# A fused attention and feed-forward kernel: tiles of x and g at another place modulo 512 bytes, and a gate ahead of GpSimd's first sums

## The chip, the core and the metric

The kernel runs on one NeuronCore of a Trainium2 chip. The engines named here are PE (TensorE, the matrix unit), DVE (VectorE), ACT (ScalarE), POOL (GpSimd) and SP (SyncE, which issues every DMA of this kernel). Each has its own instruction stream, worked off in order; they wait for each other through semaphores. The metric is the time of one execution on the device in microseconds (us), the median of several runs.

## The reference

Attention within chunks of 64 tokens, and on its output a feed-forward layer with a gated activation. All inputs are float32, except that the weights come as float64 words to this kernel.

```python
scores = scale * np.matmul(q_c, k_c.transpose(0, 1, 2, 4, 3))     # 8 batches, 8 heads, 9 chunks of 64 x 64
attn = np.exp(scores - np.max(scores, axis=-1, keepdims=True))
attn = attn / (np.sum(attn, axis=-1, keepdims=True) + 1e-09)
x = np.matmul(attn, v_c)            # rearranged to 4608 tokens x 512
...
h = x @ w_in                        # 512 x 2048
g = h * (1.0 / (1.0 + np.exp(-1.702 * h)))
return (g @ w_out)                  # 2048 x 512
```

## The kernel before, in words

**Splitting.** A float32 product is made of three matmuls in the type fp32r: each operand is split into a high part (`_h`) and a low part (`_l`), and high by low, high by high and low by high are summed in PSUM. The traces show these operands as f32.

**Tiling.** The 4608 tokens are 9 blocks of 512 (index n), and the 2048 inner features 16 slices of 128 (index j). One step g = 16 n + j of the feed-forward is: h, 12 matmuls with a 128x128 piece of `w_in` as the stationary operand and 512 columns of x as the moving one (L1513 to L1515); GELU and the high part of g on ACT (L1537, L1538); its low part on DVE (L1543); then o, for each of four 128-token tiles three matmuls with 128 columns of g as the stationary operand and 512 columns of `w_out` as the moving one (L1553 to L1555). Steps 0 and 1 do h in two halves of 256 columns (L1526 to L1529).

**Stages.** Blocks 0 to 2 go this way. For blocks 3 to 8 the product with `w_in` is done two blocks at a time with seven products for eight (L820 to L822), on tiles that lie in the weights' old places; blocks 7 and 8 do the same for `w_out` (L1067 to L1069, 256 columns wide). Sums of `w_in` pieces for this are made on POOL (`whole` and `sums`, L699 to L709) and stored to a tensor in DRAM, from where they are loaded again later.

**Weights.** A slice j of both weights arrives as 8-byte words (`raw_j`, two DMAs of SP, L365 and L370), is turned into float32 by two passes on ACT (L374, L381) and two on DVE (L387, L394), and is split by ACT (L410) and DVE (L413). The result is one tile w_j of 8 KB in each partition. That goes on during blocks 0 and 1.

**Attention.** It runs beside the feed-forward, two 128-token tiles at a time: DVE transposes, 64x64 matmuls (L1293, L1367), softmax on DVE and ACT, and one multiplication on POOL (L1323).

**Order.** The order of all 2,693 steps is written out by name in the table `ORDER`; `Plan.emit` runs through it and issues the steps' instructions. Names: `h0_g` and `h_g` the halves of h, `gh_g` and `gl_g` the parts of g, `o_g_t` the output matmuls, `raw_j`, `wsc_j`, `wlow_j`, `wshift_j`, `wj_j`, `wh_j`, `w_j` the steps of a weight, `pa0_p`, `pa_p`, `psum_p` the sums on POOL. A step's `need` only asserts that the needed steps stand ahead of it in the table. What an engine waits for on the chip follows from the tiles that its instructions read and write.

**Places.** Tiles are laid out one behind the other in each partition. Of the kernel before, in bytes modulo 512: the tiles w_j begin at 128, x_h and x_l at 128, g_h and g_l at 128. Every piece of them that a matmul reads begins a multiple of 512 bytes further on.

Of the kernel before, what the change touches and what calls it, by code (L numbers as in the profile page):

```python
# [234 lines left out]
def tile_chunk_attention_ffn(  # L235
# [9 lines left out]
    nc = tc.nc  # L245
# [38 lines left out]
    ps_a = ctx.enter_context(tc.tile_pool(name="ps_a", bufs=1, space=bass.MemoryType.PSUM))  # L284

    ident = const.tile([P, P], F32, tag="ident", name="ident")
    make_identity(nc, ident)

    buffers = {b: 2 for b in ("hp", "att", "x", "ob")}
    buffers.update({f"w{j}": 1 for j in range(NF)})  # L290
# [1403 lines left out]
```

## Time and profile before

| | us |
|---|---|
| median of 3 runs (819.7 to 821.64) | 819.97 |
| the profiled execution | 821.13 |
| its span, from the first to the last instruction | 819.4 |

The trace gives each instruction's start and duration, and for an idle stretch of an engine what ended it. A matmul's duration includes the time its results take to drain, so durations of neighbours overlap; what a matmul costs in a row of them is the distance from its start to the next one's start. The chain that ended last is followed back from the end of the program, at each step to what released the instruction or to the one before it on its engine: what stands on it sets the end. The granted TensorE clock is 1.00 in every stretch of this execution.

### The profile page before, as it was taken

Reading aid. Unit: us, or ns where it says so; the run is one execution under the profiler, and the core shown is the slowest. Engines: PE = TensorE matmul, PEld = TensorE weight load, DVE = VectorE, ACT = ScalarE, POOL = GpSimd, SP = SyncE. Lnnn points to the kernel's source line nnn. Section 1 sums busy time; section 2 is a strip of 40 time slices with the busy share of each in tenths; the row PEclk is TensorE's granted clock in tenths of the full one; section 3 lists DMA queues with packets and bytes.
Section 4 is the critical chain, followed back from the end, with each engine's and each line's share of the span. In section 5 each row is a group of like instructions: output and inputs, shape, how many; then the busy total and the mean of one; then the engine's idle time right before and its main releaser. Section 6 shows DMA issues by size and latency. Waiting matters only on the chain.

```text
span 819.4 us, 15635 instructions
## 1 busy us (share of the span) xinstructions
PE 807.3 (99%) x6038; PEld 680.4 (83%) x6038; DVE 586.2 (72%) x865; ACT 383.5 (47%) x603; POOL 91.5 (11%) x82
## 2 busy tenths in 40 slices
PE   7899999999999999999999999999999999999998
PEld 6788878888888888888888888888888888889998
DVE  5788976356475879885698898776887454569852
ACT  5899824244355536423554352422565311267430
POOL 1000170000063661000001010000000000000000
PEclk9999999999999999999999999999999999999999
DMA  9998645353266677767666437686633047673433
GB/s 242 282 297 244 167 129 123 88 128 72 57 182 174 158 199 207 186 173 219 171 172 167 104 92 193 180 211 198 164 104 116 1 130 213 194 207 118 142 92 103
DMA packets 244010, 131.08 MB, mean 160 GB/s; under 512 B 187104, under 2 KB 211680, under 8 KB 243936
## 3 DMA queue, kind: packets, MB, share of 16 engines
q1 hardware_dynamic: 243936, 130.08, 58.6%
q8 instruction: 48, 0.79, 0.4%
q14 instruction: 26, 0.21, 0.1%
HBM read 97.52 MB, written 32.51 MB: 159 GB/s over the span
## 4 chain that ended last, share of the span: by engine, by line
PE 88%; DVE 4%; SPq 3%; ACT 2%; DMA 2%; issue 1%; DVEq 0%; ACTq 0%
PE po L1553 12%; PE po L1555 12%; PE po L1554 12%; PE hp L820 9%; PE hp L822 9%; PE hp L821 9%; PE hp L1515 4%; PE hp L1513 4%; PE hp L1514 4%; SPq L470 2%; PE s L1293 2%; PE x L1367 2%; DMA w<-seven 1%; DVE wtmp L394 1%; PE acc_X L1069 1%; PE acc_X L1068 1%
## 5 line engine op out<-in xcount | busy, mean ns | idle before, releaser
L1553 PE MATMUL po<-w,g_l 128*128 128x512 f32 x448 | 176.8, 395 | 0.6 <-DVE g_l L1543 0.5
L1555 PE MATMUL po<-w,g_h 128*128 128x512 f32 x448 | 174.5, 390 | 0.0
L1554 PE MATMUL po<-w,g_h 128*128 128x512 f32 x448 | 174.5, 389 | 0.0
L1553 PEld LDWEIGHTS po<-w,g_l 128*128 128x128 f32 x448 | 84.1, 188 | 20.1 <-DVE g_l L1543 1.9
L1555 PEld LDWEIGHTS po<-w,g_h 128*128 128x128 f32 x448 | 84.1, 188 | 17.7
L1554 PEld LDWEIGHTS po<-w,g_h 128*128 128x128 f32 x448 | 84.1, 188 | 16.8
L820 PE MATMUL hp<-w,w 128*128 128x512 f32 x224 | 87.6, 391 | 0.3 <-DMA w<-seven 0.2
L1342 DVE STREAM_TRANSPOSE eT<-e 32x512 f32<-32x512 f32 x120 | 84.2, 702 | 4.4 <-POOL e L1323 2.4
L822 PE MATMUL hp<-w,w 128*128 128x512 f32 x224 | 87.2, 389 | 0.0
L821 PE MATMUL hp<-w,w 128*128 128x512 f32 x224 | 87.1, 389 | 0.0
L1323 POOL TENSOR_TENSOR e<-e,r 128x1024 f32<-128x1024 f32 x16 | 31.2, 1953 | 437.8 <-DVE r L1320 365.0
L1513 PE MATMUL hp<-x_l,w 128*128 128x512 f32 x184 | 72.0, 391 | 0.0
L1515 PE MATMUL hp<-x_h,w 128*128 128x512 f32 x184 | 71.6, 389 | 0.0
L1514 PE MATMUL hp<-x_h,w 128*128 128x512 f32 x184 | 71.6, 389 | 0.0
L1543 DVE TENSOR_TENSOR g_l<-hp,g_h 128x512 fp32r<-128x512 f32 (+1 forms) x50 | 33.2, 664 | 51.9 <-ACT g_h L1538 51.8
L1537 ACT ACTIVATE hp<-hp 128x512 f32<-128x512 f32 (+1 forms) x50 | 28.4, 569 | 66.5 <-PE hp L1515 57.3
L820 PEld LDWEIGHTS hp<-w,w 128*128 128x128 f32 x224 | 42.0, 188 | 10.5 <-issue 1.1
L822 PEld LDWEIGHTS hp<-w,w 128*128 128x128 f32 x224 | 42.1, 188 | 8.8
L821 PEld LDWEIGHTS hp<-w,w 128*128 128x128 f32 x224 | 42.1, 188 | 8.6
L820 PE MATMUL hp<-w,pieces 128*128 128x512 f32 x112 | 43.8, 391 | 0.0
L822 PE MATMUL hp<-w,pieces 128*128 128x512 f32 x112 | 43.6, 389 | 0.0
L821 PE MATMUL hp<-w,pieces 128*128 128x512 f32 x112 | 43.6, 389 | 0.0
(237 smaller groups left out, 1558.6 us busy)
## 6 DMA issues: line engine op xcount, KB each, us to landing
w<-seven SPq DMA_DIRECT2D x112, 256.0 KB, 3.3
pieces<-seven SPq DMA_DIRECT2D x56, 256.0 KB, 3.4
seven<-w SPq DMA_DIRECT2D x24, 512.0 KB, 3.8
raw<-in_moe_w_in_dram SPq DMA_DIRECT2D x16, 512.0 KB, 5.9
raw<-in_moe_w_out_dram SPq DMA_DIRECT2D x16, 512.0 KB, 6.3
four<-four_w SPq DMA_DIRECT2D x32, 256.0 KB, 3.2
raw<-in_q_dram SPq DMA_DIRECT2D x208, 32.0 KB, 2.4
raw<-in_k_dram SPq DMA_DIRECT2D x208, 32.0 KB, 2.2
```

Source lines behind the costliest of these rows:

```text
L820: nc.tensor.matmul(hp, w[:, 0, c], xl[:, c], start=c == 0, stop=False)
L821: nc.tensor.matmul(hp, w[:, 0, c], xh[:, c], start=False, stop=False)
L822: nc.tensor.matmul(hp, w[:, 1, c], xh[:, c], start=False, stop=c == 1)
L1323: nc.gpsimd.tensor_tensor(st["e"], st["e"], bc(st["r"]), op=ALU.mult)
L1342: nc.vector.transpose(st["et"][po : po + 32, :, 32 * a : 32 * a + 32], st["e"][pi : pi + 32, :, 32 * b : 32 * b + 32],)
L1513: nc.tensor.matmul(hp, wh, xl, start=cc == 0, stop=False)
L1514: nc.tensor.matmul(hp, wh, xh, start=False, stop=False)
L1515: nc.tensor.matmul(hp, wl, xh, start=False, stop=cc == NCC - 1)
L1543: nc.vector.tensor_tensor(gl[:, c], hp, gh[:, c].bitcast(F32), op=ALU.subtract)
L1553: nc.tensor.matmul(po, gl[:, c], w[:, 0, :], start=first, stop=False)
L1554: nc.tensor.matmul(po, gh[:, c], w[:, 0, :], start=False, stop=False)
L1555: nc.tensor.matmul(po, gh[:, c], w[:, 1, :], start=False, stop=last)
```

## The change

Three things change.

1. Places. x tiles and g tiles get 64 bytes more than they use, and spacers of 64, 192 and 2 times 32 bytes are laid between pools of tiles. Bytes modulo 512 in the changed program: w_j as before at 128; x_h of the blocks 0 and 2 at 192, x_l of these at 256, x_h and x_l of block 1 at 320 and 384; the two buffers of g_h at 192 and 256, those of g_l at 320 and 384. Working tiles behind them (`wtmp`, `ob` and what shares their place) move to 448. The tiles of blocks 3 to 8 that lie in the weights' places stay at 128, and so do the loaded pieces.
2. A gate. One POOL instruction of a single column reads the low half of the last weight slice w_15; the first step of every pair's sums asks for it in the table, and on POOL all sums stand behind it.
3. The table `ORDER` is written anew, over all its length. The number of PE steps is the same.

```diff
@@ ORDER @@
-    "... hp0_8 o_13_3 gh_14 o_13_2 pa0_2 pout1_0 ... s_8 pa0_0 pout0_1 pa_0 ..."
+    "... hp1_8 w_15 gate s_8 qk_1_1_10 pa0_2 o_14_0 pout0_7 xh_7 pa0_0 ..."
@@ tile_chunk_attention_ffn @@
+    const.tile([P, 16], F32, tag="gap0", name="gap0")
...
+    def x_tile(tag, name):
+        t = const.tile([P, NCC * BT + 16], F32R, tag=tag, name=name)
+        return t[:, : NCC * BT].rearrange("p (n t) -> p n t", n=NCC)
+
+    def g_tile(w, name):
+        if "gap" not in held:
+            held["gap"] = two.tile([P, 8], F32, tag="gap2", name="gap2")
+        return two.tile([P, BT + 16], F32R, tag=f"g{w}", name=name)[:, :BT]
...
-        plan.add(POOL, 1.3, rank, lambda: whole(0), need=[w0, f"w_{NF - 1}"], make=e("pa0"), take=["tmp"])
+        plan.add(POOL, 1.3, rank, lambda: whole(0), need=[w0, "gate"], make=e("pa0"), take=["tmp"])
...
-                x_h[n] = const.tile([P, NCC, BT], F32R, tag=f"xe{2 * n % 4}", name=f"x_h_{n}")
-                x_l[n] = const.tile([P, NCC, BT], F32R, tag=f"xe{2 * n % 4 + 1}", name=f"x_l_{n}")
+                x_h[n] = x_tile(f"xe{2 * n % 4}", f"x_h_{n}")
+                x_l[n] = x_tile(f"xe{2 * n % 4 + 1}", f"x_l_{n}")
+                if n == 1:
+                    const.tile([P, 48], F32, tag="gap1", name="gap1")
...
-                gh = two.tile([P, BT], F32R, tag="gh", name=f"g_h_{g}")
-                gl = two.tile([P, BT], F32R, tag="gl", name=f"g_l_{g}")
+                gh = g_tile("h", f"g_h_{g}")
+                gl = g_tile("l", f"g_l_{g}")
...
+    def gate():
+        t = const.tile([P, P], F32, tag="gate", name="gate")[:, :1]
+        w = wt[NF - 1][:, 1, 1, :1].bitcast(F32)
+        nc.gpsimd.tensor_tensor(t, w, w, op=ALU.add)
...
+    plan.add(POOL, 0.12, -80, gate, need=[f"w_{NF - 1}"], make="gate")
```

POOL's own order, before, from the attention multiplication for tile 6 on; `e` is the softmax tile, `whole` and `sums` those of the weights' sums:

```order
L1323 TENSOR_TENSOR e_1019<-e_1019,r_1061 128x1024
L699 TENSOR_TENSOR whole_1301<-w_664 128x512
L699 TENSOR_TENSOR whole_1301<-w_716 128x512
L699 TENSOR_TENSOR whole_1383<-w_289 128x512
L699 TENSOR_TENSOR whole_1383<-w_448 128x512
L706 TENSOR_TENSOR sums_1400<-whole_1301 128x256
```

and in the changed program, where the line numbers are 10 to 18 higher:

```order
L1333 TENSOR_TENSOR e_1012<-e_1012,r_1057 128x1024
L1651 TENSOR_TENSOR gate<-w_1315 128x1
L709 TENSOR_TENSOR whole_1394<-w_670 128x512
L709 TENSOR_TENSOR whole_1401<-w_307 128x512
L709 TENSOR_TENSOR whole_1401<-w_449 128x512
L709 TENSOR_TENSOR whole_1394<-w_730 128x512
L716 TENSOR_TENSOR sums_1442<-whole_1394 128x256
```

The same four `whole` instructions of the pairs 2 and 0 now follow the gate, which reads w_15 (`w_1315`); before, nothing held them until w_15 was there.

SP's queue near the start, before; `raw_368` and `raw_385` are the words of the weights 2 and 3, `rows` the q and k of tile 4, `first_b` the v of tiles 2 and 3:

```order
L365 DMA raw_237<-in_moe_w_in_dram 128x4x128
L370 DMA raw_237<-in_moe_w_out_dram 128x512
L470 DMA rows_260<-in_q_dram 128x8x64
L470 DMA rows_260<-in_k_dram 128x8x64
L470 DMA first_b_245<-in_v_dram 128x8x64
L470 DMA first_b_314<-in_v_dram 128x8x64
L365 DMA raw_368<-in_moe_w_in_dram 128x4x128
L370 DMA raw_368<-in_moe_w_out_dram 128x512
```

and in the changed program:

```order
L366 DMA raw_236<-in_moe_w_in_dram 128x4x128
L371 DMA raw_236<-in_moe_w_out_dram 128x512
L480 DMA first_b_255<-in_v_dram 128x8x64
L480 DMA first_b_252<-in_v_dram 128x8x64
L366 DMA raw_329<-in_moe_w_in_dram 128x4x128
L371 DMA raw_329<-in_moe_w_out_dram 128x512
L480 DMA rows_359<-in_q_dram 128x8x64
L480 DMA rows_359<-in_k_dram 128x8x64
```

The words of weight 2 move ahead of the two loads of `rows`.

## Rows read from the trace of the kernel before

**Rows 1.** The page: busy us of each engine with its share of the span and its instructions; the granted clock in 40 equal slices, in tenths; the chain that ended last, by engine.

```profile
PE 807.3 (99%) x6038; PEld 680.4 (83%) x6038; DVE 586.2 (72%) x865; ACT 383.5 (47%) x603; POOL 91.5 (11%) x82
PEclk9999999999999999999999999999999999999999
PE 88%; DVE 4%; SPq 3%; ACT 2%; DMA 2%; issue 1%; DVEq 0%; ACTq 0%
```

**Rows 2.** The chain that ended last in order of time, in the stretches 20 to 40 us and 91 to 125 us: start us, us, what (`issue` is a wait for nothing the profile shows).

```profile
23.82 6.60 DMA raw<-in_moe_w_out_dram
...
103.53 2.23 DVE w L413
...
112.45 0.59 DVE g_l L1543
113.08 0.50 PE po L1553
113.58 0.23 PE po L1554
113.81 0.24 PE po L1555
```

**Rows 3.** The timeline of PE in the stretch 150 to 153 us: start us, us, engine, line, operation, out<-in, shapes (stationary, then output).

```profile
150.17 0.39 PE L1553 MATMUL po<-w,g_l 128*128 128x512 f32 x1
...
150.85 0.39 PE L1513 MATMUL hp<-x_l,w 128*128 128x512 f32 x1
...
152.89 0.39 PE L1513 MATMUL hp<-x_l,w 128*128 128x512 f32 x1
```

**Rows 4.** The same view at 740 us, where the matmuls are 256 columns wide.

```profile
740.09 0.28 PE L1067 MATMUL acc_Y<-w,w 128*128 128x256 f32 x1
...
741.89 0.28 PE L1067 MATMUL acc_Y<-w,w 128*128 128x256 f32 x1
```

**Rows 5.** The same view from 217 us, where o matmuls follow a block of 64x64 matmuls of the attention.

```profile
216.79 0.59 PE L1367 MATMUL x<-eT,v 64*64 64x64 f32 x28
217.31 0.50 PE L1553 MATMUL po<-w,g_l 128*128 128x512 f32 x1
217.65 0.39 PE L1554 MATMUL po<-w,g_h 128*128 128x512 f32 x1
217.88 0.40 PE L1555 MATMUL po<-w,g_h 128*128 128x512 f32 x1
218.12 0.39 PE L1553 MATMUL po<-w,g_l 128*128 128x512 f32 x1
218.34 0.40 PE L1554 MATMUL po<-w,g_h 128*128 128x512 f32 x1
218.58 0.39 PE L1555 MATMUL po<-w,g_h 128*128 128x512 f32 x1
218.81 0.39 PE L1553 MATMUL po<-w,g_l 128*128 128x512 f32 x1
```

**Rows 6.** The same view at 30 us, where h of the first step is done in halves of 256 columns.

```profile
30.30 0.28 PE L1528 MATMUL hp<-x_l,w 128*128 128x256 f32 x1
...
31.13 0.28 PE L1529 MATMUL hp<-x_h,w 128*128 128x256 f32 x1
```

**Rows 7.** Stretches of the span, for the instructions of L1553 alone (three rows) and of L1513 alone (two rows): stretch, its us, PE busy (instructions), PEld busy (instructions), granted clock, DMA share, GB/s.

```profile
22.00:113.00 91.00, 20.78 (x52) 9.76 (x52) 1.00 0.83 235
113.00:320.00 207.00, 54.98 (x139) 26.09 (x139) 1.00 0.53 135
320.00:700.00 380.00, 101.00 (x257) 48.24 (x257) 1.00 0.57 157
22.00:113.00 91.00, 20.61 (x52) 9.75 (x52) 1.00 0.83 235
113.00:320.00 207.00, 51.35 (x132) 24.78 (x132) 1.00 0.53 135
```

**Rows 8.** Stretches of the span, all engines: stretch, its us, busy us (instructions) of PE, PEld, DVE, ACT and POOL, granted clock, DMA share, GB/s.

```profile
40.00:80.00 40.00, 39.87 (x296) 32.34 (x295) 34.50 (x38) 37.59 (x46) 1.91 (x1) 1.00 0.99 274
113.00:320.00 207.00, 206.92 (x1739) 171.49 (x1740) 130.03 (x176) 90.94 (x138) 62.28 (x59) 1.00 0.53 135
320.00:640.00 320.00, 319.80 (x2292) 263.22 (x2291) 256.58 (x406) 141.30 (x239) 14.09 (x7) 1.00 0.60 163
```

**Rows 9.** The timeline of DVE (five rows), then of POOL (four rows), from 99 to 135 us.

```profile
99.69 1.23 DVE L394 CUSTOM_DVE_ANT_0 wtmp<-raw,wtmp 128x2048 uint16<-128x2048 uint16 x1
100.83 1.22 DVE L413 TENSOR_TENSOR w<-wtmp,w 128x1024 fp32r<-128x1024 f32 x1
...
103.53 2.23 DVE L413 TENSOR_TENSOR w<-wtmp,w 128x1024 fp32r<-128x1024 f32 x1
...
106.88 1.70 DVE L394 CUSTOM_DVE_ANT_0 wtmp<-raw,wtmp 128x2048 uint16<-128x2048 uint16 x1
...
112.95 1.20 DVE L413 TENSOR_TENSOR w<-wtmp,w 128x1024 fp32r<-128x1024 f32 x1
...
102.13 2.55 POOL L699 TENSOR_TENSOR whole<-w 128x512 f32<-128x512 f32 x2 [13.39 <-DVE w L413]
105.84 3.90 POOL L699 TENSOR_TENSOR whole<-w 128x512 f32<-128x512 f32 x2 [1.16 <-DVE w L413]
...
119.52 0.74 POOL L709 TENSOR_TENSOR sums<-whole,sums 128x256 f32<-128x256 f32 x1
...
133.47 1.90 POOL L1323 TENSOR_TENSOR e<-e,r 128x1024 f32<-128x1024 f32 x1 [10.60 <-ACT hp L1537]
```

More of the change, by code (lines that the diff above doesn't have):

```diff
@@ L865, in high @@
             g = (g1 if late else g0) + h
-            g_t[g] = [two.tile([P, BT], F32R, tag=f"g{w}", name=f"g_{w}_{g}") for w in "hl"]
+            g_t[g] = [g_tile(w, f"g_{w}_{g}") for w in "hl"]
             nc.scalar.activation(g_t[g][0], words(h, late), AF.Copy)
@@ L1022, in pair @@
             if r < 2:
-                return [two.tile([P, BT], F32R, tag=f"g{w}", name=f"c_{w}_{q}_{p}") for w in "hl"]
+                return [g_tile(w, f"c_{w}_{q}_{p}") for w in "hl"]
             t = wt[slots[r - 2]][:, 0]
```

344 rows, old and new, of the table ORDER are left out of this document.

## The prediction

> **What bounds the kernel now.** I read the page first: PE is busy in 99% of the span, 88% of the chain that ended last is PE's, and the granted clock is at its upper level in all 40 slices [rows 1]. So no engine beside PE can be the bound over the whole run; the time can only come out of the matmuls themselves, or out of the stage in which the chain is not PE's. Second, that chain in order of time: before 113.08 us it passes through the weights' words (a DMA of 6.60 us), ACT and DVE, for instance a split of w on DVE of 2.23 us; from 113.08 us on it is one matmul after the other [rows 2]. Third, the stretches: from 40 to 80 us the DMA engines are busy for 0.99 of the time and ACT for 37.59 of 40 us, from 113 us on DVE, ACT and POOL have room (130 of 207 us for DVE, 257 of 320 later) and the DMA share is 0.53 to 0.60 [rows 8]. A matmul that gets shorter after 113 us therefore shortens the run; one that gets shorter before mostly waits longer for its weight.
>
> Last, what a matmul costs. At 150 us twelve of them take 152.89 - 150.17 = 2.72 us, 226.7 ns each for 512 columns [rows 3]. At 740 us fifteen take 741.89 - 740.09 = 1.80 us, 120.0 ns each for 256 columns [rows 4]. The difference, 106.7 ns for 256 columns, is 0.417 ns per column, the upper clock level. What is left over is 13.3 ns per matmul at either width, though every one of them has another stationary operand. It is not quite constant: in the 256-column start of the kernel seven take 31.13 - 30.30 = 0.83 us, 118.6 ns each, a rest of 11.9 [rows 6], and after a break five take 218.81 - 217.65 = 1.16 us, 232 ns each, a rest of 18.7 [rows 5]. The columns cost the same in all three places, so something beside the columns, which depends on how a matmul stands to the weight load under it, costs 12 to 19 ns.
>
> **The change, part by part.** The sum is made against the profiled execution, 821.1 us; the median of the runs is 820.0, 1.2 lower.
>
> *Places.* In the kernel before, every stationary and every moving operand of a product has the same place modulo 512 bytes. The change pulls them apart for L1513 to L1515 (w against x) and L1553 to L1555 (g against w). After 113 us L1513 has 132 matmuls and L1553 139 + 257 [rows 7]; times three lines each, 3 x 528 = 1584. Before 113 us there are 3 x (52 + 52) = 312 more. The seven-products stage (L820 to L822, L1067 to L1069) keeps its places, so nothing is taken off there. No row of the kernel before has operands at two different places, so the price is bounded: at most the whole rest goes, 13.3 ns; at least nothing; and below nothing, since the 232 ns after a break show that the same operands can also run 5.3 ns slower than steady [rows 3, 5]. I take 8 ns, a bit over half of 13.3: the rest moves with the phase between load and columns, from 11.9 to 18.7, which speaks for two reads that get in each other's way, but a turn from an o matmul to an h matmul still loads w while w streams, and some fixed part for changing the weights may stay. 1584 x 8 ns = 12.7 us. On the 312 early ones I count nothing: DMA and ACT hide it [rows 8]. If that cover weren't there, they would be worth 312 x 8 ns = 2.5 us more.
>
> A rule of the Trainium skill bears on the size. Its page "TensorE: Matmul & The Clock Gate", section "Back-to-back issue gap", puts a matmul of a warm array at its columns over 2.4 GHz and about 2.5 ns, some 216 ns for 512 columns. The row says 226.7, so this kernel is 11 ns slower than that rule; were all of it the places' doing, the gain would be an estimated 17 us and the time about 801.
>
> *The gate.* POOL's `whole` additions run beside the weights' last passes. While they run, DVE's L413 takes 2.23 us against 1.22 just before, and L394 1.70 against 1.23 [rows 9]: 1.01 + 0.47 = 1.5 us, in the stretch where the chain goes through DVE. With the gate the sums start only after the last split (112.95 + 1.20 = 114.15 us) [rows 9]. Bounds are 0 and 1.5; I take 1.0, since part of a DVE stall there is found again as a wait for the next words. On the other side, POOL does four `whole` additions (2.55 us for two, undisturbed) and two rounds of sums behind the gate, where before only the sums stood there, which ended at 119.52 + 0.74 = 120.26. About 5.1 us later is 125.4, and POOL's next work, the multiplication of the attention, began at 133.47 after 10.60 us of idling [rows 9], so 8 us of cover are there; without it up to 5 us of attention delay would result, in a stage where PE has other steps. The gate itself is one column on an idle engine: nothing. The DVE passes beside the moved sums get longer after 114 us, where DVE has 77 us of room in 207 [rows 8].
>
> *The order.* On SP the words of weight 2 pass two `rows` loads. Words stand on the chain with 6.60 us for one DMA [rows 2]. The gain lies between 0 and about 2 us (two loads of 256 KB each at the 274 GB/s of the full stretch are 2 x 262144 / 274e9 = 1.9 us [rows 8]), and the `rows` come as much later, for an attention step that could become a wait. I take 0.5. The rest of the table is re-sorted with the same number of PE steps; PE idles so little (819.4 - 807.3 = 12 us in all [rows 1], most of it before the first weight is there) that I give this nothing, within 2 us to either side.
>
> Sum: 821.1 - 12.7 - 1.0 - 0.5 = 806.9; less 1.2 for the median, 805.7, so 806. Its own range, with 5 to 11 ns per matmul, is 801 to 811.
>
> **Rivals.**
>
> *The place does nothing.* Then the 13.3 ns are what it costs to change the weights. For it: they are equal at 512 and 256 columns [rows 3, 4], where a clash of reads could have grown with the time that both run. Against it: the rest is not one number (11.9, 13.3, 18.7) [rows 3 to 6]. Only gate and order are left: 821.1 - 1.5 - 1.2 = 818.4, within 816 to 821 for the unknown of the order.
> The same page of the Trainium skill, in "Step-by-step: what each phase is for", says that TensorE has two independent read ports into SBUF and that loading the next weights takes no read bandwidth from the running matmul. By that rule this rival is what must happen, at 818 us. The rows neither confirm nor refute it, since all places are equal in them.
>
> *Part of it.* Only a few of the pairs of places help (the distances are 64, 128, 192 and 256 bytes), and the mean gain is 1 to 4 ns. 1584 x 2.5 ns = 4 us: 821.1 - 4 - 1.5 - 1.2 = 814, within 810 to 816.
>
> *Slower: the rhythm is lost.* After a break the spacings are 231 to 236 ns until they fall into 227 [rows 5]. The steady 226.7 may be a rhythm in which the load's reads and the columns' reads of the same place fall in step and stay out of each other's way. With operands at four different distances, which change from matmul to matmul, no such rhythm forms, and the matmuls stay at 232 ns: 1584 x 5.3 ns = 8.4 us, 821.1 + 8.4 - 1.5 - 1.2 = 827. It decides from a spacing of about 228.3 ns on, where 1584 x 1.7 ns eat up the 2.7 us that gate, order and the step to the median are worth. For it: the one stretch that is out of rhythm is slower with the same operands. Against it: the early 256-column stretch is out of that rhythm and faster [rows 6].
>
> *The change does not do what it says.* The places are fixed by the layout, and I see nothing by which a tile of L1513 or L1553 would fall back to 128; little chance, and its time is that of "does nothing".
>
> **How the numbers follow.** Forecast 0.40; part of it 0.09; does nothing 0.30; rhythm lost 0.21. A measurement of this kernel tells about 0.3%, 2.5 us, from no change: 817.5 to 822.5. The forecast (0.40), the partial gain (0.09) and a sixth of "does nothing" (0.05, where the gate's and order's gain are at their upper bounds) are faster: 0.54. Of "does nothing" 0.22 stay within, with 0.01 of the last rival: 0.23. Slower are 0.20 of the last rival and 0.03 of "does nothing", where the new order costs its 2 us and more: 0.23. The range reaches down to 798, nearly the whole 13.3 ns (1584 x 13.3 = 21 us: 821.1 - 21.1 - 1.5 - 1.2 = 797), and up to 824, which takes in "does nothing" and the near part of the last rival; what is left out is some 0.15 above and 0.03 below.
>
> **What would show it.** The spacing of L1553 to L1555 and of L1513 to L1515 in blocks 0 to 2: about 219 ns by the forecast, 226.7 if the place does nothing, 228 to 232 if the rhythm is lost. The seven products of L820 to L822 and L1067 to L1069 must stay at 227 and 120; if they change too, it wasn't the place. L413 and L394 near 105 us at 1.2 us, no `whole` before the last split, and PE alone on the chain from 111 or 112 us on would show the gate right. I would be wrong if the spacings don't move and the time still falls (the order did it), if the gain per matmul holds but PE idles after 113 us on ACT or DVE, or if the seven products wait longer for their pieces.

## The result, and the profile after

The changed kernel takes 829.61 us (median of 3 runs, 829.04 to 830.34) where the kernel before takes 819.97: a ratio of 1.0105 (1.0091 to 1.0118), slower. The range on record ended at 824; of the cases on record it is the rival that was given 0.21 and 827 us.

The page of the changed kernel, for the rows of [rows 1]: the engines, the granted clock, and the chain that ended last.

```profile
PE 816.7 (99%) x6038; PEld 681.4 (82%) x6038; DVE 586.8 (71%) x865; ACT 381.1 (46%) x603; POOL 91.2 (11%) x83
PEclk9999999999999999999999999999999999999999
PE 95%; DVE 2%; ACT 1%; DMA 1%; SPq 0%; issue 0%; POOL 0%; DVEq 0%; POOLq 0%
```

PE makes the same 6038 matmuls at the same clock and is busy for 9.4 us longer. Its share of the chain rises from 88 to 95%. In order of time the chain passes to PE not at 113 us, as in [rows 2], but at 38 (start us, us, what).

```profile
36.75 0.61 DVE qkT L1279
...
37.38 0.60 ACT qkT L1276
...
38.03 1.16 PE s L1303 x64
39.19 0.43 PE hp L1525
39.62 0.23 PE hp L1526
```

From there on PE waits for no weight. That comes from the order and the gate, not from the slower matmuls: in the run below with order and gate and the old places the chain passes to PE at 37.9 us too (first two rows), in the one with the new places alone at 113.6 us (last two).

```profile
37.23 0.61 ACT qkT L1273
...
37.88 1.16 PE s L1300 x64
...
112.95 0.59 DVE g_l L1555
113.58 0.50 PE po L1565
```

The timeline of PE at 150 us, in the columns of [rows 3]; twelve matmuls of 512 columns take 152.92 - 150.13 = 2.79 us, 232.5 ns each instead of 226.7.

```profile
150.13 0.39 PE L1525 MATMUL hp<-x_l,w 128*128 128x512 f32 x1
150.35 0.39 PE L1526 MATMUL hp<-x_h,w 128*128 128x512 f32 x1
150.59 0.40 PE L1527 MATMUL hp<-x_h,w 128*128 128x512 f32 x1
150.82 0.39 PE L1565 MATMUL po<-w,g_l 128*128 128x512 f32 x1
...
152.92 0.39 PE L1525 MATMUL hp<-x_l,w 128*128 128x512 f32 x1
```

The products that kept their places did not change where no displaced matmul stands ahead of them. Fifteen matmuls of L830 to L832 take 333.43 - 330.03 = 3.40 us, 226.7 ns each, and fifteen of L1077 to L1079 751.04 - 749.24 = 1.80 us, 120.0 ns each, as in [rows 4]. One part of that stage did move, against what the prediction says: 96 of the 672 matmuls of L1077 to L1079 take their stationary operand (`c_h`, `c_l`) from the g tiles. They take 117.9 ns instead of 119.9, and the stage from its first to its last start 80.3 us instead of 80.5.

```profile
330.03 0.39 PE L831 MATMUL hp<-w,w 128*128 128x512 f32 x1
...
333.43 0.39 PE L831 MATMUL hp<-w,w 128*128 128x512 f32 x1
```

```profile
749.24 0.28 PE L1077 MATMUL acc_Y<-w,w 128*128 128x256 f32 x1
...
751.04 0.28 PE L1077 MATMUL acc_Y<-w,w 128*128 128x256 f32 x1
```

After the break near 219 us, five o matmuls take 221.62 - 220.46 = 1.16 us, 232 ns each, as they did in [rows 5]. There such spacings soon gave way to a steady 227; here the matmuls go on at a mean of 232 to 233. What was a state of passage is the steady one.

```profile
220.46 0.39 PE L1566 MATMUL po<-w,g_h 128*128 128x512 f32 x1
...
221.62 0.39 PE L1525 MATMUL hp<-x_l,w 128*128 128x512 f32 x1
```

The stretch of [rows 8] from 113 to 320 us holds 1722 matmuls instead of 1739, with PE busy throughout:

```profile
113.00:320.00 207.00, 207.00 (x1722) 167.96 (x1721) 130.54 (x172) 90.83 (x139) 65.75 (x64) 1.00 0.53 133
```

The splits near 105 us take 1.2 us, and POOL's sums stand behind the last of them, as the gate asks (for [rows 9]):

```profile
99.08 1.23 DVE L414 TENSOR_TENSOR w<-wtmp,w 128x1024 fp32r<-128x1024 f32 x1 [0.48 <-ACT w L411]
...
105.52 1.18 DVE L414 TENSOR_TENSOR w<-wtmp,w 128x1024 fp32r<-128x1024 f32 x1
...
114.86 1.23 DVE L414 TENSOR_TENSOR w<-wtmp,w 128x1024 fp32r<-128x1024 f32 x1 [0.53 <-ACT w L411]
...
116.17 0.19 POOL L1651 TENSOR_TENSOR gate<-w 128x1 f32<-128x1 f32 x1 [27.90 <-DVE w L414]
116.31 5.02 POOL L709 TENSOR_TENSOR whole<-w 128x512 f32<-128x512 f32 x4
...
134.51 1.91 POOL L1333 TENSOR_TENSOR e<-e,r 128x1024 f32<-128x1024 f32 x1 [10.16 <-DVE r L1330]
```

All neighbours among the matmuls of 512 columns in this trace can be sorted by two places: where the first one's moving operand begins, and where the stationary operand of the second one begins, which is loaded while the first one streams. Mean distance from start to start, without those over 260 ns (waits):

| moving, next stationary (bytes mod 512) | pairs | mean ns |
|---|---|---|
| 128, 128 | 1065 | 228.5 |
| 128, 192 / 256 / 320 / 384 (o) | 437 / 440 / 182 / 188 | 232.7 / 234.2 / 229.8 / 232.4 |
| 192 / 256 / 320 / 384, 128 (h) | 204 / 118 / 105 / 64 | 231.9 / 230.1 / 232.3 / 233.0 |
| other pairs (from an h to an o) | 58 | 234.3 |

The displaced 1796 pairs have a mean of 232.5 ns: 5.8 ns more than 226.7, 10.4 us in all. The pairs at equal places suffer too, 1.8 ns each or 1.9 us; of the 308 among them at 229 ns or more, 277 are one of the first six matmuls behind a displaced pair or a break. These 12.3 us are counted from 226.7; the kernel before has a mean of 227.0 over the same neighbours, so against it they are 11.4 us. They are less in the span, since some of it stands where PE waited for weights before and since gate and order give something back.

The table sorts neighbours; it does not show that the next stationary operand is the one that counts. In 68 neighbours the first is a seven-products matmul, with both of its operands at 128, and the next is an o matmul, so that the table has them as displaced: their mean is 227.5 ns. In another 68 the first is an o matmul, with g displaced from `w_out`, and the next a seven-products matmul, and the table has them as equal: 234.6 ns. The price begins with the first matmul whose own two operands stand apart.

### The profile page after: what moved, and what is told of

The parts are those of the page before. It is cut to its first block, busy times and chain, and to the rows that moved or that the text cites. A ratio compares the mean times of both kernels' runs of the same rounds, so it can differ in the third digit from the quotient of the medians.

```text
span 827.3 us, 15637 instructions
## 1 busy us (share of the span) xinstructions
PE 816.7 (99%) x6038; PEld 681.4 (82%) x6038; DVE 586.8 (71%) x865; ACT 381.1 (46%) x603; POOL 91.2 (11%) x83
## 4 chain that ended last, share of the span: by engine, by line
PE 95%; DVE 2%; ACT 1%; DMA 1%; SPq 0%; issue 0%; POOL 0%; DVEq 0%; POOLq 0%
PE po L1565 13%; PE po L1567 13%; PE po L1566 12%; PE hp L830 9%; PE hp L831 9%; PE hp L832 9%; PE hp L1527 5%; PE hp L1526 5%; PE hp L1525 5%; PE s L1303 2%; PE x L1377 2%; PE acc_X L1078 1%; PE acc_X L1077 1%; PE acc_X L1079 1%; PE acc_Y L1079 1%; PE acc_Y L1078 1%
## 5 line engine op out<-in xcount | busy, mean ns | idle before, releaser
L1565 PE MATMUL po<-w,g_l 128*128 128x512 f32 x448 | 179.3, 400 | 0.0
L1567 PE MATMUL po<-w,g_h 128*128 128x512 f32 x448 | 177.0, 395 | 0.0
L1566 PE MATMUL po<-w,g_h 128*128 128x512 f32 x448 | 176.9, 395 | 0.0
L1566 PEld LDWEIGHTS po<-w,g_h 128*128 128x128 f32 x448 | 84.3, 188 | 18.7
L830 PE MATMUL hp<-w,w 128*128 128x512 f32 x224 | 87.5, 391 | 0.0
L832 PE MATMUL hp<-w,w 128*128 128x512 f32 x224 | 87.4, 390 | 0.0
L1527 PE MATMUL hp<-x_h,w 128*128 128x512 f32 x184 | 72.8, 396 | 0.0
L1526 PE MATMUL hp<-x_h,w 128*128 128x512 f32 x184 | 72.5, 394 | 0.0
L830 PEld LDWEIGHTS hp<-w,w 128*128 128x128 f32 x224 | 42.0, 188 | 9.8 <-issue 0.3
L832 PEld LDWEIGHTS hp<-w,w 128*128 128x128 f32 x224 | 42.0, 188 | 9.0
L832 PE MATMUL hp<-w,pieces 128*128 128x512 f32 x112 | 43.7, 390 | 0.0
L830 PE MATMUL hp<-w,pieces 128*128 128x512 f32 x112 | 43.7, 390 | 0.0
```

Source lines behind the costliest of these rows:

```text
L830: nc.tensor.matmul(hp, w[:, 0, c], xl[:, c], start=c == 0, stop=False)
L832: nc.tensor.matmul(hp, w[:, 1, c], xh[:, c], start=False, stop=c == 1)
L1526: nc.tensor.matmul(hp, wh, xh, start=False, stop=False)
L1527: nc.tensor.matmul(hp, wl, xh, start=False, stop=cc == NCC - 1)
L1565: nc.tensor.matmul(po, gl[:, c], w[:, 0, :], start=first, stop=False)
L1566: nc.tensor.matmul(po, gh[:, c], w[:, 0, :], start=False, stop=False)
```

## The experiments

The theory was that the distance between the place of the moving operand and that of the next stationary one, modulo 512, sets what a matmul costs, and that equal places are the cheapest. Its rivals: the new order makes PE meet other engines' accesses; only a distance that *changes* from matmul to matmul costs; 128 is a good place by itself.

**The two halves of the change.** One kernel is the changed one without its spacers and paddings, the other the kernel before with them:

```diff
-    const.tile([P, 16], F32, tag="gap0", name="gap0")
...
-        t = const.tile([P, NCC * BT + 16], F32R, tag=tag, name=name)
+        t = const.tile([P, NCC * BT], F32R, tag=tag, name=name)
...
-        if "gap" not in held:
-            held["gap"] = two.tile([P, 8], F32, tag="gap2", name="gap2")
-        return two.tile([P, BT + 16], F32R, tag=f"g{w}", name=name)[:, :BT]
+        return two.tile([P, BT], F32R, tag=f"g{w}", name=name)[:, :BT]
...
-                if n == 1:
-                    const.tile([P, 48], F32, tag="gap1", name="gap1")
```

Order and gate alone:

> The changed kernel with its order and its gate, all tiles of x and g back at 128 modulo 512. Theory 'place' (a matmul that streams from another place than the next stationary operand is loaded from costs some 5 ns more): the spacing is 226.7 ns again everywhere, and the time is that of before less the 0.8 us by which the first products ran ahead, 818 to 820 us. Theory 'order' (the new table makes PE meet other engines' accesses): the spacings of 229 to 236 ns stay, and the time is 828 to 830 us.

819.26 us, 0.9974 of before (0.9962 to 0.9986). The timeline of PE gives back the old spacing, (152.66 - 149.94) / 12 = 226.7 ns:

```profile
149.94 0.39 PE L1520 MATMUL hp<-x_l,w 128*128 128x512 f32 x1
...
152.66 0.39 PE L1560 MATMUL po<-w,g_l 128*128 128x512 f32 x1
```

Places alone:

> The kernel before with the new places alone: its old order and no gate. Theory 'place': spacings of 229 to 236 ns in L1525 to L1527 and L1565 to L1567, 829 to 831 us. Theory 'order': 226.7 ns and 820 us.

832.04 us, 1.0122 of before (1.0106 to 1.0138), with (152.84 - 150.04) / 12 = 233 ns in the old order:

```profile
150.04 0.40 PE L1565 MATMUL po<-w,g_l 128*128 128x512 f32 x1
...
152.84 0.39 PE L1525 MATMUL hp<-x_l,w 128*128 128x512 f32 x1
```

Of the change as a whole, the places cost 10 us, and order and gate win about 2 back (1.5 us in the repeat below). The order is not the cause.

**Matmuls alone.** A kernel that has only rows of matmuls, each with its stationary operand at one place and the moving one at another:

```diff
+    def group(pairs, width=512, count=COUNT):
+        for i in range(count):
+            a, m = pairs[i % len(pairs)]
+            s = s_t[a][:, 128 * (i % 4) : 128 * (i % 4) + 128]
+            b = (step[0] // 3) % 4
+            nc.tensor.matmul(acc[b][:, :width], s, m_t[m][:, :width], start=step[0] % 3 == 0, stop=step[0] % 3 == 2)
+            step[0] += 1
```

> Only rows of matmuls, 36 of each kind, with nothing beside them; attention and feed-forward are left out, and the output is one tile of sums stored 36 times. All tiles lie at 128 modulo 512 plus the number in their name; s is the stationary operand, m the moving one. Theory 'distance': equal places give 226.7 ns at 128 as at 192, 256, 320 and 384; every other distance gives more, each its own figure between 228 and 236 ns, in a row of one distance too. Rival 'change of distance' (only a distance that changes from matmul to matmul breaks the rhythm): each row of one distance falls into 226.7 ns, and only the mixed rows at the end lie above. Rival 'absolute place' (128 is good by itself): the rows with both operands at 192 to 384 lie above 227 ns as well. Rival 'neighbours' (the extra comes from the other engines' accesses to these places): all rows give the same.

> Rows of matmuls again, 30 of each kind, at the distances that the run before left out (8 to 248 bytes at 512 columns, multiples of 16 and some others at 256); attention and feed-forward are left out and the output is one tile of sums stored 36 times. Theory 'modulo 256' (the extra depends on the distance modulo 256, and no place is better than the same place at 512 columns): every row of 512 columns lies between 226.7 and 237 ns, and only distance 0 gives 226.7. Rival 'a better place exists': some distance gives under 226 ns at 512 columns, as 192 bytes gave 113.3 ns against 120.0 at 256 columns. At 256 columns the rows around 192 bytes show how wide that better place is: 113.3 at 192 alone, or from 176 to 208.

Mean spacing over the last 20 matmuls of each row, from the starts in the two traces (- where no row was run):

| moving minus stationary, bytes | 512 columns, ns | 256 columns, ns |
|---|---|---|
| 0 | 226.7 | 120.0 |
| 8 / 12 / 20 | 233.2 / 228.8 / 240.0 | 120.0 / - / - |
| 64 | 228.8 | 117.8 |
| 112 | 231.2 | 113.3 |
| 128 | 233.3 | 118.7 |
| 192 | 233.3 | 113.3 |
| 248 | 230.0 | - |
| 256 | 226.7 | 120.0 |
| 320 | 228.8 | 117.8 |
| 384 | 232.4 | - |
| 448 | 233.3 | - |

Three stretches of the first of these kernels, each one row of 36 weight loads (stretch, its us, PEld busy and its instructions, granted clock, DMA share, GB/s), at distance 64, at 320 and at equal places of 192:

```profile
57.85:66.08 8.23, 6.76 (x36) 1.00 0.00 0
107.91:116.15 8.24, 6.76 (x36) 1.00 0.00 0
132.93:141.13 8.20, 6.76 (x36) 1.00 0.00 0
```

The last row is 8.20 / 36 = 227.8 ns over all of its matmuls: the first ten or so behind a change of place take 224 to 236 ns, until the steady spacing is reached.

No other engine works there, so the extra is TensorE's own. Distances 0 and 256 give 226.7, 64 and 320 the same 228.8, 192 and 448 the same 233.3; only 128 and 384 differ, by 0.9 ns, and the last run below shows 128 at 232.4 as well. So it is the distance modulo 256 that counts, not 512. Equal places at 192, 256, 320 and 384 give 226.7 too, so 128 is no better than another. At 512 columns none of the 39 distances tried is better than 0; the worst, 20 and 120, take 240.0 ns, more than the 237 expected. At 256 columns 0 is among the worst, and 112 and 192 give 6.7 ns less. Rows of one distance keep their price, so it is not the change alone; but change costs by itself: three matmuls at distance 0 and one at 64 in turn have a mean of 232.3 ns, above both 226.7 and 228.8.

One mixed row speaks against the theory's choice of the two operands. Stationary and moving operand stand at 0 and 64 in one matmul and at 64 and 0 in the next, so that each moving operand has the place of the next stationary one. By the theory that is distance 0 throughout; the mean is 231.7 ns, near the 231 that the matmuls' own distances have on average (228.8 for 64 and 233.3 for -64). In a row of one distance both readings are the same. Which reads meet in the engine, no run here shows.

**The places of the changed kernel, alone.**

> Matmuls alone again: the places of 400 successive matmuls of the changed kernel (from 172 us on, where they take 232.4 ns each), then 40 at equal places, then half of the sequence with every other place put to 256 bytes; the rest is left out and the output is one tile of sums stored 36 times. If the places alone set the time, the first stretch gives 232 to 233 ns with no other engine at work, the last one 226.7. If the other engines' accesses have a part in it, the first lies nearer to the mean of the single distances weighted by their number, about 230.5 ns, or lower.

Windows as above, over the 400 matmuls, the 40 at equal places, and the 200 of which the last is not in the window:

```profile
23.88:116.89 93.01, 75.18 (x400) 1.00 0.00 1
116.90:125.95 9.05, 7.51 (x40) 1.00 0.00 0
125.96:171.00 45.04, 37.31 (x199) 1.00 0.00 0
```

93.01 / 400 = 232.5 ns; in the changed kernel the same 400 take 232.4. The last stretch, with 256 bytes in place of every displacement, is back at 226.7 from start to start. The places set the time alone. But the table's prices do not add up to it: their mean over the 400 distances is 230.9 ns, and the neighbours of distance 0 among them, moving to next stationary, take 232.5 as all the others do. In a mixture the sequence as a whole has a price, not the single pair.

**One place for all.**

```diff
-    const.tile([P, 16], F32, tag="gap0", name="gap0")
+    const.tile([P, 64], F32, tag="gap0", name="gap0")
...
-        t = const.tile([P, NCC * BT + 16], F32R, tag=tag, name=name)
+        t = const.tile([P, NCC * BT], F32R, tag=tag, name=name)
...
-            held["gap"] = two.tile([P, 8], F32, tag="gap2", name="gap2")
-        return two.tile([P, BT + 16], F32R, tag=f"g{w}", name=name)[:, :BT]
+            held["gap"] = two.tile([P, 32], F32, tag="gap2", name="gap2")
+        return two.tile([P, BT], F32R, tag=f"g{w}", name=name)[:, :BT]
...
-                    const.tile([P, 48], F32, tag="gap1", name="gap1")
+                    const.tile([P, 64], F32, tag="gap1", name="gap1")
```

> The changed kernel with its order and gate, but all tiles of x and g at one place, 256 bytes from the weights' (384 modulo 512). Theory 'distance modulo 256': as if the places were equal, 226.7 ns steady and 819 to 820 us. Theory 'modulo 512' (any difference costs): 229 to 236 ns and 826 to 831 us.

One run, 822.85 us, against one of 820.78 for before on that chip: the steady spacing is 226.7 again, the time is some 3 us above what was expected of it and above order and gate with the old places. The waits of PE from 355 to 370 us and from 400 to 410 us (waited for: us in total, times, longest) name 2.6 us of that:

```profile
PE hp L830 <- DMA w<-seven: 1.6, 1, 1.6
...
PE hp L830 <- DMA w<-seven: 1.0, 1, 1.0
```

The pieces of the seven-products stage come from DRAM late there. With order and gate alone the same wait took 0.9 us; in the changed kernel there is none of that size, and PE arrives nearly 5 us later. So part of a gain ahead of 350 us can be given back at this point. The rest of the 3 us is the start: the first product began at 22.5 us here and at 21.1 us there.

> The same with one place 64 bytes beyond the weights' (192 modulo 512). By the rows of the run with matmuls alone, h then has distance 64 (228.8 ns, +2.1) and o distance 448 (233.3 ns, +6.6): 396 x 2.1 + 1188 x 6.6 = 8.7 us after 113 us, 827 to 829 us, L1525 to L1527 nearer to 229 and L1565 to L1567 nearer to 233 ns. If only a change of distance costs, 820 us.

One run, 829.85 us. The o pairs (448) have a mean of 233.0 ns, as in the table; the h pairs (64) 231.3 and not 228.8. Between h and o the distance changes, and the mixed row above shows that change costs; that this is the whole of the 2.5 ns was not tried. The time is 0.9 us above the upper end of what was expected by the price list.

**Gate and order apart.**

```diff
-        plan.add(POOL, 1.3, rank, lambda: whole(0), need=[w0, f"w_{NF - 1}"], make=e("pa0"), take=["tmp"])
+        plan.add(POOL, 1.3, rank, lambda: whole(0), need=[w0, "gate"], make=e("pa0"), take=["tmp"])
...
+    plan.add(POOL, 0.12, -80, gate, need=[f"w_{NF - 1}"], make="gate")
```

> The kernel before with the gate alone (its old table with one name more, old places). In the run with order and gate together PE is 1.16 us ahead of before from 50 to 98 us and another 1.1 us from 98 to 124 us, where the sums on GpSimd no longer stand beside the last splits. If that second part is the gate's, this kernel is about 1 us faster than before (0.1%, about 820 where before is 821), its splits L413 take 1.2 us, and PE is even with before up to 98 us. If the table does it all, this kernel equals before.

> The new table alone, old places, no gate. If the two parts add up, 1.2 us faster than before by the early start (0.15%), with splits of over 2 us where GpSimd's sums run beside them; if the gate is the whole gain, equal to before.

> Order and gate together, old places, against its two parts on one chip: 0.9974 of before again (2 us), the sum of the two parts.

All three came out at 0.9982 of before (0.9973 to 0.9991): 819.94, 819.92 and 819.90 us against 821.42. They don't add up. The gate alone makes the splits short, and so does the new order alone, where POOL's `whole` stands beside other work. The first two rows are DVE with the gate alone, the last three DVE and POOL with the order alone:

```profile
104.52 1.23 DVE L413 TENSOR_TENSOR w<-wtmp,w 128x1024 fp32r<-128x1024 f32 x1
106.87 1.22 DVE L394 CUSTOM_DVE_ANT_0 wtmp<-raw,wtmp 128x2048 uint16<-128x2048 uint16 x1
```

```profile
105.14 1.18 DVE L413 TENSOR_TENSOR w<-wtmp,w 128x1024 fp32r<-128x1024 f32 x1
...
100.69 1.29 POOL L706 TENSOR_TENSOR whole<-w 128x512 f32<-128x512 f32 x1 [11.54 <-DVE w L413]
106.47 3.79 POOL L706 TENSOR_TENSOR whole<-w 128x512 f32<-128x512 f32 x3 [4.50 <-DVE w L413]
```

Counted by products, PE gains 1.1 us on before between 98 and 124 us in each of these traces, which fits one stall that either edit takes away. The head start of the first products is no part of the change: with order and gate the first product began at 21.1 us in the one execution and at 22.7 in the other.

**The price list used the other way.**

```diff
+            read[q, p] = wt[slots[r - 2]].rearrange("p m h f -> p (m h f)")
...
+            if (q, p) in read:
+                gh, gl = [read[q, p][:, 512 * i + 16 :][:, :512] for i in range(2)]
```

> Order and gate with the old places, but in the last stage (L1077 to L1079, 256 columns) the stationary operand is read 64 bytes further on in 576 of the 672 matmuls, so that the moving one stands 192 bytes beyond it modulo 256; these matmuls take their 128 columns 16 further on than they should, so the output of blocks 7 and 8 is not the reference's, and nothing else changes. The rows of matmuls alone gave 113.3 ns against 120.0 at this distance. Theory 'modulo 256, whatever the sign': 113.3 ns in these 576, and 576 x 6.7 = 3.9 us less than the same kernel with all places equal (0.9974 to 0.9982 of before): 0.993, 815 to 816 us. If only the one arrangement of that run gives it (moving operand at 192 modulo 512), 117 to 120 ns and at most 1.7 us.

0.9966 of before (0.9952 to 0.9981), 818.36 us. That is within the interval of order and gate alone (0.9962 to 0.9986), so the time by itself shows no gain. The last stage, its 671 spacings added up, is 1.7 us shorter (78.8 us instead of 80.5). In six of its seven products the displaced matmuls take 117.8 ns, in one 113.3 (11.30 us and 10.86 us for 96 each):

```profile
745.45:756.75 11.30, 11.30 (x98) 11.30 (x97) 11.30 (x19) 8.39 (x15) 0.00 (x0) 1.00 0.39 138
790.79:801.65 10.86, 10.86 (x98) 10.86 (x97) 2.58 (x5) 0.63 (x1) 0.00 (x0) 1.00 0.17 50
```

So the same distance gave two spacings, and neither theory had foreseen that.

> Matmuls alone: distances of 192, 448, 64 and 320 bytes at 256 columns, each entered from distance 0, 64 and 128 and from matmuls of 512 columns, and 64, 192 and 448 at 512 columns entered from 0, 32 and 128; the rest is left out and the output is one tile of sums stored 36 times. Theory 'modulo 256 with two rhythms': 192 and 448 show 113.3 ns or 117.8 ns at 256 columns, according to what stood before. Theory 'modulo 512': 192 always gives 113.3 and 448 always 117.8. At 512 columns one figure per distance if the spacing is the distance's own, several if the entry decides there too.

Distance 192 entered from rows of 256 columns, and entered from matmuls of 512; then the same for 448:

```profile
24.68:28.76 4.08, 4.08 (x37) 1.00 0.02 4
43.98:48.20 4.22, 4.22 (x36) 1.00 0.00 0
50.37:54.45 4.08, 4.08 (x37) 1.00 0.00 0
69.67:73.89 4.22, 4.22 (x36) 1.00 0.02 4
```

After the first few, the starts are 113.3 ns apart in the first and third, 117.8 in the second and fourth: 448 behaves as 192, and what stood before decides between two steady spacings. It does not decide alone: entered from distance 0 at 256 columns, a moving operand 448 beyond the stationary one came to 113.3, but a stationary operand 64 beyond the moving one, which is the same distance modulo 512, held 117.8. And a stationary operand 192 beyond the moving one (320, or 64 modulo 256) held 113.3, where a moving operand at 64 or 320 held 117.8 from every entry. At 512 columns, 64, 192 and 448 gave 228.8, 233.3 and 233.3 from whichever of three rows they were entered; 128 ran at 232.4 in the three rows here and at 233.3 in the first kernel. Whether 192 instead of 64 bytes in the last stage gives the faster rhythm was not tried.

## Why the prediction was wrong

*Places: the step that failed.* "I take 8 ns, a bit over half of 13.3" had the wrong sign. The displaced matmuls take 5.8 ns more. The argument was that a rest which moves with phase (11.9, 13.3, 18.7 ns) means two reads in each other's way, and that pulling the operands apart takes them out of it. The first half is not shown; the second doesn't hold: at equal places the rest of 13.3 ns is the least of 39 distances at 512 columns. The early row at 118.6 ns [rows 6], which spoke for it, was a row of 256 columns, and there equal places are indeed poor. A reading at one width was carried to the other. So the step that failed is the price of the places, put at 8 ns less per matmul, and the runs showed 5.8 ns more in its place.

*The rival "the rhythm is lost"* had sign, place and price: 5.3 ns by the spacings after a break [rows 5] (231, 236, 228, 233 and 230 ns, not all of them from 231 to 236), 5.8 measured; 827 us, 829.6 measured. What it left out is the 1.9 us of the equal pairs behind a displaced one and part of the early matmuls. Of its mechanism one part fell: no change of distance is needed for it, a single distance has its price in a steady row. That the steady 226.7 of before is a state which a disturbance breaks for some matmuls was right: rows of equal places take 224 to 236 ns at first. Why the reads stay out of each other's way at some distances and not at others, no run shows.

*The bounds.* "At least nothing; and below nothing, since the 232 ns after a break show that the same operands can also run 5.3 ns slower" was on the page as the lower end, and the range stopped inside it. The row after the break was the only one that the prediction has of 512 columns out of the steady state, and it said slower.

*"The place does nothing"*, and with it the page "TensorE: Matmul & The Clock Gate" of the Trainium skill, section "Step-by-step: what each phase is for", by which loading weights takes nothing from the running matmul: the rows of matmuls alone differ by up to 13.3 ns (226.7 to 240.0) with the place alone, so for these 4-byte operands the two reads are not without effect on each other. The 216 ns, which the same page's "Back-to-back issue gap" gives for a matmul by itself, were reached at no distance; nor were the about 131 ns that it gives for a stream of weight loads and matmuls.

*The gate* was put at 1.0 us and gave 1.1 between 98 and 124 us, and its cover held: POOL's next work began at 134.5 us in the changed kernel. *The order* was put at 0.5 us for SP's words; no such gain could be told from the scatter of the start, and what the order gives in the time is the gate's gain over again (0.9982 by either). *The early matmuls*, counted at nothing, did cost in the kernel with places alone: before 98 us its products fell 0.8 us behind those of before.

The kernel with order and gate and the old places is faster than both (0.9974 and 0.9982 in two measurements); the gate alone reached the same.

## What to carry to other kernels

For matmuls like these, each with another stationary operand, the place of stationary and moving operand modulo 256 bytes is worth up to 13 ns per matmul of 512 columns, and it has to be measured: a row of 30 matmuls for each distance, at the width that the kernel uses, is a price list. A full kernel that keeps to one place for its tiles came within 1 us of it; with mixed distances the real sequence has to be run, which cost 1.6 ns per matmul more than the list. Tiles whose sizes are multiples of 256 bytes, laid end to end, stand at distance 0, which was the best at 512 columns. In a trace, the few matmuls after a break are a free experiment: they show the same instructions out of their steady state. And a chain that looks different after a change of several parts says nothing about which part did it, until each has run alone.

## What the runs showed of the hardware

- In rows of one distance the spacing of fp32r matmuls depends on the distance of moving and stationary operand modulo 256 bytes, from 226.7 to 240.0 ns at 512 columns, with other prices 8 bytes further on (228.8 at 12, 240.0 at 20). At 128 two steady spacings were seen, 232.4 and 233.3.
- At 256 columns the order is another: 120.0 at distance 0, 113.3 at 112 and 192. At 192, 320 and 448 two steady spacings, 113.3 and 117.8, were seen; what ran before, and which of the two operands stands further on, both had a part in it.
- With a distance that alternates between 64 and -64, so that each moving operand stands where the next stationary one does, the mean is 231.7 ns and not 226.7.
- One displaced matmul in four raised the mean of all four from 226.7 to 232.3 ns.
